# An attention and SwiGLU kernel on one core: fewer, longer dummy products, F's turns and V's projections moved up, a quotient moved to GpSimd, and smaller weight loads at the start

## The chip, the cores and the metric

The kernel runs on one core of one Trainium2 chip. The metric is the device time of one execution in microseconds (us). All runs here are of one core; the granted clock of every run is 0.997 to 1.0. Three runs, with three different kernels, fell to 0.997 at 570.4 to 570.9 us.

The engines are called by the profile's names: PE is TensorE (PEld its weight loads), DVE is VectorE, ACT is ScalarE, POOL is GpSimd, SP is SyncE. GpSimd computes the attention's quotients and also issues nearly all loads.

## The reference

```python
k_proj = np.einsum('ks,bhsd->bhkd', E, k)          # q, k, v: 8 x 8 x 1024 x 64, E, F: 64 x 1024
v_proj = np.einsum('ks,bhsd->bhkd', F, v)
attn   = softmax(q @ k_proj.T / sqrt(64))          # over 64 projected keys
x      = (attn @ v_proj), heads side by side       # 8192 x 512
out    = (silu(x @ w_gate) * (x @ w_val)) @ w_out  # d_ff = 1536
```

## The kernel before

There are 8 batches of two halves of 512 tokens. Steady work is the feed-forward network: per half, 12 features of 128 columns, each with four gate and four value products of 128x512. The attention of the coming half is put into "slots" between them. Only the first batch's attention and its loads can't hide, and the change is all there.

Some words used below: a "turn" is a transpose, done as a product with the identity on TensorE (`u_T` for q, `u_A` for the attention, `turn` for E and F). "Quotient" N(b, u) is the exponentials times the reciprocal of their sum (`u_N`). BD and BDV hold the projected keys and values, AT the turned attention, xT the attention's result; "P V" is the product of attention and projected V. "Gate 1" or "value 4-5" is the load of these features' weights. A load "lands" when its semaphore says that it is complete. An "instruction packet" is a DMA packet that brings the program's own instructions (queue q8 in the profile).

```python
def load_w_gv(c0, c1, which=(0, 1)):      # weights of features c0..c1-1, GpSimd issues
    cs = slice(c0 * P, c1 * P)
    for wsrc, wdst in [((moe_w_gate, wg), (moe_w_val, wv))[i] for i in which]:
        nc.gpsimd.dma_start(out=wdst[:, :, cs], in_=wsrc[:, cs].rearrange(...))

def u_N(b, u, eng=nc.gpsimd):             # the attention's quotient, on GpSimd
    ... eng.tensor_tensor(out=a, in0=ee, in1=rr, op=ALU.mult)

def u_TD(b, ch):                          # q of later batches is transposed by DMA
    nc.sync.dma_start_transpose(out=t[:], in_=qb[b, ch][:]...)

def place(b):                             # slots of batch b's attention
    ...
    put(s0 + (9 if b == 2 else -6), u_TD, b, 0)
    o = 14 if b == 2 else 6
    sa = [s0 + o + 3 * j for j in range(NJ)]       # scores, and quotient one slot later
...
load_w_gv(4, 6)                           # the loads after the start, in this order
load_q(0, 1, hs=(0, 4))
load_w_gv(6, 8)
load_q(0, 1, hs=(4, 8))                   # q's heads 4-7 of the second half
load_w_gv(8, 10); load_w_gv(10, 12)
load_q(1, 0); load_k(1); load_wo(0); load_wo(1)
for i, u in enumerate(range(4, 8)):       # the second half of batch 0
    put(11 + i, u_T, 0, u)                # q's turn on TensorE
    put(13 + i, u_S, 0, u)                # scores
    put(14 + i, u_R, 0, u); put(14 + i, u_N, 0, u)
```

The softmax here doesn't subtract the row's maximum and nothing guards it: scores larger than these inputs give would overflow.

## Time and profile before

| | before |
|---|---|
| median time | 568.79 us (568.78 to 568.80, 3 runs) |
| span of the profiled run | 566.9 us |
| TensorE busy | 560.2 us, 99% |
| first full-width product (feature 2, gate) | 25.07 us |
| from there to the end | 541.8 us |

The table is read from the bottom: after 25 us TensorE does almost nothing but multiply. The prediction below shows the lines.

### The profile page before, as it was taken

To read this page: it belongs to the slowest core of one execution; us is meant where nothing else is said; L and a number is where in the kernel's file an instruction comes from. 1 tells how busy PE (TensorE), PEld (TensorE's weight loads), DVE (VectorE), ACT (ScalarE), POOL (GpSimd) and SP (SyncE) were. 2 spreads that over 40 slices of the span, in tenths; PEclk is the share of its full clock that TensorE was granted. 3 is DMA by queue.
4 is the path that set the end of the run, shared out by engine and by line. 5 is a ranking of instruction groups with operands and counts; after the bars stand their busy time and mean duration, and the time that the engine had idled before them with its cause. 6 is when DMAs were issued, how large, how long until landed. Compare 5 with 4: busy or idle time off the path is not lost.

```text
span 566.9 us, 7938 instructions
## 1 busy us (share of the span) xinstructions
PE 560.2 (99%) x2970; PEld 266.3 (47%) x2970; DVE 339.2 (60%) x576; ACT 236.0 (42%) x417; POOL 110.4 (19%) x124
## 2 busy tenths in 40 slices
PE   8999999999999999999999999999999999999997
PEld 4654444444444444444444444444444444444444
DVE  3786664766476645766466655666547665545550
ACT  3664352444435433443434434354343543443222
POOL 6851250124012400124002230023100220000000
PEclk9999999999999999999999999999999999999999
DMA  9999989729913795029940499105990214100012
GB/s 201 194 200 188 175 126 199 141 57 187 192 50 74 113 196 119 38 57 163 183 83 37 76 185 204 38 19 101 200 183 20 57 38 75 38 37 32 25 38 93
DMA packets 111159, 62.78 MB, mean 111 GB/s; under 512 B 64272, under 2 KB 102416, under 8 KB 111120
## 3 DMA queue, kind: packets, MB, share of 16 engines
q0 software_dynamic: 42896, 29.49, 36.1%
q1 hardware_dynamic: 67392, 31.46, 26.2%
q10 hardware_dynamic: 832, 1.31, 0.8%
q8 instruction: 23, 0.38, 0.3%
q14 instruction: 16, 0.13, 0.1%
HBM read 60.29 MB, written 16.78 MB: 136 GB/s over the span
## 4 chain that ended last, share of the span: by engine, by line
PE 97%; ACT 1%; DVE 1%; issue 0%
PE gps L377 29%; PE yps L415 29%; PE vps L377 29%; PE kvp L150 3%; PE sc L271 2%; PE pv L328 2%; PE warm L513 1%; ACT ee L275 0%; ACT AT L138 0%; DVE BD L138 0%; ACT th L389 0%; PE qTp L237 0%; PE efp L501 0%; PE aTp L317 0%; PE pv L343 0%
## 5 line engine op out<-in xcount | busy, mean ns | idle before, releaser
L396 DVE SCALAR_TENSOR_TENSOR s<-th,gps 128x512 f32<-128x512 f32 x192 | 130.3, 679 | 134.4 <-ACT th L389 134.0
L377 PE MATMUL gps<-xT,wg 128*128 128x512 bf16 (+1 forms) x776 | 197.6, 377 | 0.1
L377 PE MATMUL vps<-xT,wv 128*128 128x512 bf16 (+1 forms) x776 | 197.5, 377 | 0.0
L415 PE MATMUL yps<-wo,hT 128*128 128x512 bf16 (+1 forms) x780 | 194.5, 376 | 0.0
L389 ACT ACTIVATE th<-gps 128x512 f32<-128x512 f32 x192 | 114.6, 597 | 159.0 <-PE gps L377 153.9
L401 DVE TENSOR_TENSOR hT<-s,vps 128x512 bf16<-128x512 f32 x192 | 131.9, 687 | 20.4 <-DVE s L396 0.5
L301 POOL TENSOR_TENSOR AAd<-ee,rr 128x512 bf16<-128x512 f32 x56 | 58.2, 1041 | 342.5 <-issue 180.6
L415 PEld LDWEIGHTS <-hT 128*128 128x128 bf16 x780 | 76.2, 98 | 89.9
L377 PEld LDWEIGHTS <-wv 128*128 128x128 bf16 x776 | 74.0, 98 | 83.3 <-issue 2.9
L377 PEld LDWEIGHTS <-wg 128*128 128x128 bf16 x776 | 74.0, 98 | 81.3 <-issue 1.2
L425 ACT ACTIVATE ysb<-yps 128x512 f32<-128x512 f32 (+1 forms) x65 | 38.4, 590 | 77.7 <-PE yps L415 77.7
L138 ACT CAST xT<-pv 128x512 bf16<-128x512 f32 (+1 forms) x62 | 35.9, 581 | 52.5 <-PE pv L328 50.3
L286 DVE TENSOR_REDUCE zz<-ee 128x8 f32<-128x512 f32 x64 | 43.4, 679 | 22.1 <-ACT ee L275 22.1
L275 ACT ACTIVATE ee<-sc 128x512 f32<-128x512 f32 x64 | 38.2, 597 | 19.8 <-PE sc L271 18.7
L271 PEld LDWEIGHTS <-qTd 128*128 128x128 bf16 x224 | 17.2, 98 | 13.2 <-DMA qTd<-qb 0.2
L328 PE MATMUL pv<-AT,BDV 128*128 128x512 bf16 x60 | 22.4, 379 | 0.1
L271 PE MATMUL sc<-BD,qTd 128*128 128x128 bf16 x224 | 21.6, 219 | 0.0
L288 DVE RECIPROCAL rr<-zz 128x8 f32<-128x8 f32 x64 | 13.0, 203 | 6.6 <-DVE zz L286 0.5
L108 POOL DMA_DIRECT2D qb<-in_q_dram x18 | 16.3, 907 | 1.4 <-POOLq L651 0.8
L150 PE MATMUL kvp<-kb,ET 128*64 128x512 bf16 (+1 forms) x72 | 15.5, 358 | 0.0
L162 DVE CAST BDV<-kvp 64x256 bf16<-64x256 f32 x7 | 3.0, 426 | 20.0 <-ACT ks L158 17.8
L150 PE MATMUL kvp<-vb,FT 128*64 128x512 bf16 x56 | 13.4, 382 | 0.0
(66 smaller groups left out, 137.6 us busy)
## 6 DMA issues: line engine op xcount, KB each, us to landing
out_dram<-ysb SPq DMA_DIRECT2D x63, 256.0 KB, 2.3
qb<-in_q_dram POOLq DMA_DIRECT2D x14, 512.0 KB, 18.1
kb<-in_k_dram POOLq DMA_DIRECT2D x7, 1024.0 KB, 11.0
vb<-in_v_dram POOLq DMA_DIRECT2D x7, 1024.0 KB, 14.5
wo<-in_moe_w_out_dram POOLq DMA_DIRECT2D x2, 768.0 KB, 21.9
wg<-in_moe_w_gate_dram POOLq DMA_DIRECT2D x5, 256.0 KB, 8.4
wv<-in_moe_w_val_dram POOLq DMA_DIRECT2D x5, 256.0 KB, 9.0
kraw<-in_k_dram ACTq DMA_DIRECT2D x2, 512.0 KB, 4.9
```

Of the source, the lines that this page charges most:

```text
L138: (nc.scalar.copy if eng is nc.scalar else eng.tensor_copy)(out=out, in_=in_)
L150: nc.tensor.matmul(out=t[lo : lo + 64, h0:h1].rearrange("p h d -> p (h d)"), lhsT=w[:, j, :], rhs=src[b][:, h0:h1, j, :], start=(j == 0), ...
L271: nc.tensor.matmul(out=ps[:, n, :], lhsT=t[:, n, :], rhs=BD[b % 2][:, 4 * g + n, :], start=True, stop=True)
L275: nc.scalar.activation(out=e[:].rearrange("p h j k -> p (h j k)"), in_=ps[:].rearrange("p a k -> p (a k)"), func=AF.Exp, scale=scale,)
L286: nc.vector.reduce_sum(out=z[:], in_=e[:], axis=AX.X)
L301: eng.tensor_tensor(out=a.rearrange("p j h k -> p h j k"), in0=ee.pop((b, u))[:], in1=rr.pop((b, u))[:].unsqueeze(3).to_broadcast([P, 4, 2 ...
L377: nc.tensor.matmul(out=ps[:, ts], lhsT=(wg, wv)[w][:, kt, f * P : (f + 1) * P], rhs=x[:, kt, ts], start=(kt == 0), stop=(kt == NKT - 1),)
L389: nc.scalar.activation(out=th[:], in_=ps[:], func=AF.Tanh, scale=0.5)
L396: nc.vector.scalar_tensor_tensor(out=s1[:], in0=th[:], scalar=1.0, in1=g[:], op0=ALU.add, op1=ALU.mult)
L401: nc.vector.tensor_tensor(out=hT[c][:, f, :], in0=s1[:], in1=ps[:], op=ALU.mult)
L415: nc.tensor.matmul(out=yy[c][:, cs], lhsT=hT[c][:, f, i * P : (i + 1) * P], rhs=wo[:, f, cs], start=(f == 0), stop=(f == NFT - 1),)
L425: nc.scalar.activation(out=ysb[:, cs], in_=yy[c][:, cs], func=AF.Copy, scale=0.5)
```

## The change

The intent: put fewer instructions into TensorE's stream with dummies of the same length (they keep its clock up), take the copies of F's turn out from between ScalarE's exponentials, project V before the first P V, free VectorE of the last quotient N(0,3) by giving it to GpSimd, and let the weights of features 2 and 3 land separately.

```diff
-        warm(11)                                # bf16, 512 columns each
+        for n in (8, 8, 6):                     # one fp32 product of 64 n columns each
+            warm(n)
         turn(0, "v")
-        warm(4)
+        warm(8)
 ...                                             # two more such places, one dummy dropped
         load_w_gv(1, 2, (1,))
-        load_w_gv(2, 4, (0,))
+        load_w_gv(2, 3)
 ...
         u_KV(0, "k", (4, 8), at="y")
-        warm(1)
+        turn(1, "a", (0,), dve)
         u_KT0((2, 4), "vg", (dve, dve, act, act))
         u_T(0, 1, "a", dve)
         u_T(0, 3, "a", dve)
+        turn(1, "a", (1,))
 ...                                             # both turn(1, ...) removed further down
         u_R(0, 3)
+        u_N(0, 3)                               # GpSimd; was u_N(0, 3, dve)
+        load_w_gv(3, 4)
         u_A(0, 0, act)
-        u_N(0, 3, dve)
         u_V0(0, 2, "y")
+        u_V0(2, 3, "v")
         u_PV2(0, 0, 0, 0, act)
-        u_V0(2, 3, "y")
-        u_A(0, 2, act)
-        u_V0(3, 4, "v")
+        u_A(0, 2, dve)
+        u_V0(3, 4, "y")
 ...
+        f_mm(0, 0, 0, 0)
         u_A(0, 3, act)
-        load_w_gv(2, 4, (1,))
-        f_mm(0, 0, 0, 0)
```

More of the change, by code (lines that the diff above doesn't have):

```diff
@@ L490 @@
         load_k(0, 4, 8)
-        zeros = const.tile([P, CW], BF16, name="zeros")
+        zero32 = const.tile([P, CW], FP32, name="zero32")
+        nc.vector.memset(zero32[:], 0.0)
+        zeros = const.tile([P, 2 * P], BF16, name="zeros")
         nc.vector.memset(zeros[:], 0.0)
@@ L495, with turn @@
         nc.vector.memset(ks[0][64:P], 0.0)
-        def turn(which, at, halves=(0, 1)):
+        def turn(which, at, halves=(0, 1), eng=nc.scalar):
             for half in halves:
@@ L506, in turn @@
                 js = slice(4 * half, 4 * half + 4)
-                copy(nc.scalar, (ET, FT)[which][:, js, :], ps[:])
+                copy(eng, (ET, FT)[which][:, js, :], ps[:])
         def warm(n):
             ps = bank("v", [P, CW], FP32, "warm")
-            for _ in range(n):
+            z = zeros if n < 4 else zero32
+            for _ in range(n if n < 4 else 1):
                 nc.tensor.matmul(
-                    out=ps[:], lhsT=zeros[:, 0:P], rhs=zeros[:],
+                    out=ps[:, 0 : min(64 * n, CW) if n >= 4 else 2 * P],
+                    lhsT=z[:, 0:P],
+                    rhs=z[:, 0 : min(64 * n, CW) if n >= 4 else 2 * P],
                     start=True, stop=True,
@@ L537 @@
         u_KT0((0, 2), "vg", (dve, dve, dve, act))
-        warm(1)
+        warm(4)
         u_S(0, 0, "g")
@@ L542 @@
         load_w_gv(1, 2, (1,))
-        load_w_gv(2, 4, (0,))
+        load_w_gv(2, 3)
         u_T(0, 2, "a", act)
-        warm(2)
+        warm(4)
         u_KV(0, "k", (4, 8), at="y")
-        warm(1)
+        turn(1, "a", (0,), dve)
         u_KT0((2, 4), "vg", (dve, dve, act, act))
@@ L553 @@
         u_N(0, 2)
-        turn(1, "a", (0,))
         u_S(0, 1, "g")
@@ L557 @@
         u_N(0, 1)
-        turn(1, "a", (1,))
         u_S(0, 3, "v")
         u_R(0, 3)
+        u_N(0, 3)
+        load_w_gv(3, 4)
         u_A(0, 0, act)
-        u_N(0, 3, dve)
         u_V0(0, 2, "y")
+        u_V0(2, 3, "v")
         u_PV2(0, 0, 0, 0, act)
-        u_V0(2, 3, "y")
-        u_A(0, 2, act)
-        u_V0(3, 4, "v")
+        u_A(0, 2, dve)
+        u_V0(3, 4, "y")
         u_PV1(0, 0, 2, 0, dve)
```

## The prediction

> **What bounds the kernel now.** I read the page first, then busy time in long stretches, then the chain of waits for the first 25 us, and last each load of the start with its time to landing. The page and the stretches say where a change can matter at all:
>
> ```profile
> span 566.9 us, 7938 instructions
> PE 560.2 (99%) x2970; PEld 266.3 (47%) x2970; DVE 339.2 (60%) x576; ACT 236.0 (42%) x417; POOL 110.4 (19%) x124
> ...
> 15.00:25.00 10.00, 8.85 (x123) 7.10 (x123) 6.95 (x15) 6.89 (x16) 8.85 (x13) 1.00 1.50 193
> 25.00:565.00 540.00, 538.75 (x2772) 252.54 (x2771) 326.71 (x547) 223.56 (x390) 90.92 (x93) 1.00 0.61 107
> ```
>
> In a stretch line the columns are the window, its length, then the busy time of PE, PEld, DVE, ACT and POOL, the granted clock, the DMA share and GB/s. From 25 to 565 us TensorE is busy 538.75 of 540 us at clock 1.00; the list of waits has no wait of TensorE over 0.1 us after 21 us. So 566.9 - 25.07 = 541.8 us after the first full-width product of feature 2 (start 25.07) is product after product, and the change touches none of it. The time moves by what the start of that product moves, one to one, as long as the loads then still arrive.
>
> In the start, the chain of waits (start, length, what) ends so:
>
> ```profile
> 14.94 0.60 ACT ee L275
> 15.54 0.26 ACT FT L138
> 15.80 0.50 ACT ee L275
> 16.30 0.26 ACT FT L138
> 16.57 0.50 ACT ee L275
> 17.07 0.48 ACT AT L138
> 17.55 0.29 ACT BDV L185
> ...
> 23.29 0.39 PE gps L377 x2
> 23.68 0.02 issue
> 23.70 0.61 ACT th L389
> 24.31 0.02 issue
> 24.33 0.70 DVE s L396
> 25.03 0.04 issue
> 25.07 0.38 PE gps L377
> ```
>
> The reader is to see ScalarE as the limit from 14.9 to 17.8: the two copies of F's turn (0.26 each) stand between the exponentials, and the first evicted attention (AT) and V projection (BDV) queue behind. At the end, tanh (0.61) and the VectorE product (0.70) free the bank that feature 2 needs.
>
> A second limit hardly shows in the chain: the loads. The share of the DMA engines is at its top from 2 us on. The landings, each from the issue line of a small window, are (issue + time to landing): V heads 0-3 at 5.66 + 9.9 = 15.5, heads 4-5 at 16.9, heads 6-7 at 18.1, gate feature 0 at 18.8, value feature 0 at 8.65 + 12.5 = 21.2, gate 1 at 11.24 + 10.1 = 21.4, value 1 at 14.26 + 7.7 = 22.0. The first use of value 0 is the product at 21.36:
>
> ```profile
> 21.36 0.60 PE L377 MATMUL vps<-xT,wv 128*128 128x256 bf16 x4
> ```
> ```profile
> wv<-in_moe_w_val_dram POOLq DMA_DIRECT2D x1, 128.0 KB, 12.5
> ```
> ```profile
> q0 software_dynamic: 818, 0.20, 172.8%
> q8 instruction: 1, 0.02, 4.9%
> ```
>
> So that weight is only 0.2 us early. Value 0 comes 2.3 us after gate 0, though the same 128 KB elsewhere take about 0.6 (gate 1 to value 1: 21.4 to 22.0). The last fence, DMA packets between 19.0 and 20.2 us, shows why I suspect this is no matter of bytes: one packet of an instruction queue, 0.02 MB, took 4.9% of 16 engines x 1.2 us, 0.94 us of one engine, in the middle of these loads. A load has landed only when all its engines are through, so that engine's lag delays value 0, gate 1 and value 1.
>
> **What the Trainium skill says.** "FP8 and Floating Point Precision", section "TensorE Precision Notes": a true fp32 product is four passes through the array. The trace agrees roughly: E's eight fp32 turns of 64 columns take 1.07 us, 133 ns each, where four passes of 64 columns at 2.4 GHz (the clock of the next page) are 107. "TensorE: Matmul & The Clock Gate", Part 1: the array starts at half clock and is released after a busy window of some 3.4 us. The trace agrees: eleven dummies of 512 columns take 4.88 us, 444 ns each, and full-width products later advance by 0.86 / 4 = 216 ns. "DMA: Bandwidth & Descriptors", "Issuing engines are not separate DMA queues": all issuers share the 16 engines; the instruction packet above fits. Its table "Specifications" puts full rate at 512 B and up; here loads of one feature (256 B packets) take about 0.74 us of data, loads of two (512 B) 1.34, so two halves cost 2 x 0.74 - 1.34 = 0.14 more.
>
> **The change, part by part.**
> Dummies: 11 + 4 + 1 + 2 + 1 = 19 products of 512 columns become 3 + 1 + 1 + 1 = 6 fp32 products of 22, 8, 4 and 4 times 64 columns. At four passes, 22 x 64 x 4 = 5632 = 11 x 512: the same time in the first group, the same for 8, 4 (for 2), and 1024 instead of 512 column passes for the first 4; the last one is gone. That extra 0.21 us falls in TensorE's 0.72 us wait for BD before 10.90: free. The memset ahead is twice as large in bytes: 0.48 us (the row of that size, BD's) instead of 0.27, so the dummies start about 0.2 us later and end near 6.1 to 6.4 instead of 6.1; E's turns start at 6.12 now, and K's copies hold the projection till 8.0 of its 8.2. Cost 0 to 0.2 us. Removed are 13 products and 13 weight loads, 26 instructions of TensorE's stream.
>
> F's turns: the first goes between k's second projection (ends 13.18; F landed at 5.00 + 8.1 = 13.1) and the kT products at 13.63, its copy on VectorE done by 13.9, when BD begins: free. The second falls where TensorE waits for BD before 14.56. Both 0.26 us copies leave the exponentials: these end near 16.5 instead of 17.1, AT at 17.0 instead of 17.55, BDV of pairs 0-1 at 17.3 instead of 17.83. That is 0.5 us.
>
> V projections ahead: pair 2 is projected at 16.9 (its V lands then), P V of pairs 0-1 at 17.4 instead of 17.88. The second attention's turn follows at 17.9, when GpSimd has its quotient (17.65), and VectorE copies it (0.4) as N(0,3), 1.13 us, has gone to GpSimd (there done at 18.7 + 1.0 = 19.7). It is ready at 18.5 instead of 19.65. Pair 3 must wait for V at 18.1; its BDV at 18.95, P V 1 of pair 3 at 19.0, its xT at 19.7. The first gate products then end at 19.9 instead of 21.14: 1.2 us of work gained up to here.
>
> Then value 0 is needed at 20.3 and, if it lands as before, is there at 21.2. From there: value 0 at 21.2 to 21.65, gate 1 to 22.1, P V to 22.3, its xT (0.58 after 0.2 of latency) at 23.05, the second gate half ends at 23.3 instead of 23.68, and tanh, product and feature 2 follow at 24.85. Gain 0.2 us. If the instruction packet no longer stands in the way, value 0 lands near 19.6, gate 1 at 20.4, value 1 at 21.1; the same steps give feature 2 at 24.0: gain 1.05.
>
> Slices: gate 2 and value 2 alone land earlier (some 0.6 us) than a load of two; features 3 and later come 0.27 us later and are issued behind N(0,3). Value 2 lands at 24.65 and is wanted at 25.93 now, gate 4 at 26.0 and 28.5, so even a start 1 us earlier has room. Cost 0.
>
> Where the instruction packet falls is the choice. It follows TensorE's instruction count; at 19.14 about 290 traced TensorE instructions have begun. The stream is 26 shorter, but the work runs up to 1.2 us ahead by then, and the two nearly cancel: I expect it at 18.9 to 19.6 again, still among the first weights. So more weight on the small gain: 0.2 (likeliest), 0.4 if the packet falls just behind value 0, 1.05 if past all four. Weighted 0.55, 0.25, 0.15 and 0.05 for a loss of 0.3: 0.35 us.
>
> **Rivals.**
> 1. The loads take over wholly (gain 0 to 0.2, 568.6 to 568.8): for it, value 0 is only 0.2 us early; against it, the packet's place is not fixed.
> 2. The packet moves out of the way: 567.7. For it, fewer TensorE instructions; against it, the earlier work.
> 3. The fp32 dummies last longer or do not count as activity, or the later memset misses the busy window: the clock rises 3.4 us later, E's turns, dummies and k's projection run at half speed. About 1.5 us more, of which some 0.9 hides behind value 0: 569.3. Against it, four passes keep the array as busy, and the dummies start 1.4 us in, still before the last 3.4 us ahead of the rise at 6.1.
> 4. VectorE becomes the limit: it already carries three reductions and reciprocals from 15.57 to 18.06, and takes a copy of F's turn and one of AT on top. Those fall at 13.5 and after 18.06, so I see at most 0.1 us.
>
> **Range and chances.** 568.79 - 0.35 = 568.4. The range takes in rival 2 at its low end and a small loss at its high end: 567.7 to 568.9. Two per cent is 11.4 us, more than nearly all that the start has to give or a cold clock could cost: within 2% is 0.985.
>
> **What would show it.** Right: the exponentials without a copy between them, ending near 16.5; first gate products ending near 19.9; then TensorE waiting for value 0 until about 21.2; feature 2 at 24.8; 541.8 us after it. Wrong: no instruction packet among the first weights and value 0 at 19.6 (rival 2); full clock only past 6.5 us, or E's turns later than 6.5 (rival 3); a TensorE wait for a weight after feature 2 (the slices come too late).

## More of the kernel before

Of the kernel before, after 19.5 us (who waited for what: us in total, times, longest):

```profile
PEld L271 <- DMA qTd<-qb: 0.2, 1, 0.2
```

It is the weight load of batch 2's first scores, which takes q as a DMA has transposed it (`qTd`), at 104.84 us; the transfer landed at 104.80. Its wait tells that the transfer came just in time, though the products show no gap.

## The result, and the profile after

The changed kernel took 568.99 us (median of 4 runs: 569.17, 569.14, 568.82, 568.84), the kernel before 568.78 in the same rounds. Ratios are the mean time of one kernel's fast runs over that of the other's of the same rounds, so not quite the ratio of the medians: 1.0004, interval 0.9986 to 1.0021. Later (r_after, chip 2) it was 568.97 (568.33 to 569.42) against 568.79, ratio 1.0003. It is the same time, or 0.2 us more, where 0.4 less was forecast. The range of 567.7 to 568.9 missed it by 0.1.

First the chain of waits of the changed kernel (start, length, what):

```profile
15.66 1.53 ACT ee L275 x3
17.19 0.48 ACT AT L138
17.67 0.28 ACT BDV L185
...
19.33 1.03 POOL AA L301
20.36 0.76 POOL wg L118
21.13 0.74 POOL wv L118
...
25.51 9.19 DMA qb<-in_q_dram
34.70 0.05 issue
34.74 0.40 PE qTp L237 x4
```

The three exponentials now stand together (1.53 us), as the change wanted. But the chain leaves the computing engines: it goes through GpSimd's last quotient (N(0,3), `AA`), then its issue of the loads one after another, then a load of q, to a turn on TensorE at 34.74. The chain of before has no load in it. Its shares by engine, from its page, and then those of after:

```profile
PE 97%; ACT 1%; DVE 1%; issue 0%
```
```profile
PE 95%; DMA 2%; POOL 1%; ACT 1%; DVE 0%; issue 0%
```

Now the stretch from feature 2's first product to 35 us, before and then after. The columns are the window, its length, then busy us of PE, PEld, DVE, ACT, POOL with instructions, clock, DMA share, GB/s:

```profile
25.07:35.00 9.93, 9.93 (x58) 5.00 (x58) 8.29 (x13) 4.51 (x9) 5.48 (x7) 1.00 1.45 196
```
```profile
24.65:35.00 10.35, 9.72 (x57) 4.82 (x57) 8.71 (x14) 4.75 (x9) 7.21 (x10) 1.00 1.36 179
```

Feature 2 starts at 24.65 instead of 25.07: the start did gain 0.42 us. But before, TensorE was busy in all of its 9.93 us, and after, in 9.72 of 10.35. The waits of the changed kernel after 19.5 us name it, for products and weight loads:

```profile
PE qTp L237 <- DMA qb<-in_q_dram: 0.6, 1, 0.6
```
```profile
PEld L237 <- DMA qb<-in_q_dram: 0.8, 1, 0.8
PEld L271 <- DMA qTd<-qb: 0.4, 1, 0.4
```

The book of starts, from the timelines of both kernels: feature 2 is 0.42 us ahead; the turn of q's heads 4-7 comes at 34.74 instead of 34.37, the line of before that follows, so the lead is a lag of 0.37. The 0.8 us between are the wait of its weight load.

```profile
34.37 0.39 PE L237 MATMUL qTp<-ident_bf,qb 128*128 128x128 bf16 x4
```

Then a wait for GpSimd's quotients near 40.7 adds some 0.1; at the first scores of batch 1 the lag is 0.49 (61.62 against 61.13), and it stays so to the end (567.4 against 566.9).

Why the load was late shows in the DMA queue. Stretches of 1 us, before and then after, same columns:

```profile
22.00:23.00 1.00, 1.00 (x12) 0.89 (x11) 0.74 (x3) 0.35 (x1) 1.00 (x2) 1.00 1.45 198
...
24.00:25.00 1.00, 0.98 (x9) 0.72 (x8) 0.67 (x1) 0.72 (x2) 0.69 (x2) 1.00 1.45 196
25.00:26.00 1.00, 0.93 (x5) 0.45 (x5) 0.90 (x3) 0.17 (x1) 0.68 (x1) 1.00 1.45 196
```
```profile
22.00:23.00 1.00, 0.98 (x10) 0.73 (x9) 0.85 (x3) 0.59 (x1) 1.00 (x2) 1.00 1.19 112
...
24.00:25.00 1.00, 0.90 (x8) 0.54 (x6) 0.90 (x2) 0.60 (x1) 1.00 (x3) 1.00 1.22 146
25.00:26.00 1.00, 1.00 (x7) 0.44 (x5) 0.99 (x2) 0.29 (x1) 1.00 (x2) 1.00 1.17 150
```

The queue moved 196 GB/s without a break before; after, it fell to 112 and then to about 150. GpSimd's timelines say why (start, length, engine, line), before and then after:

```profile
16.64 2.04 POOL L301 TENSOR_TENSOR AA<-ee,rr 128x512 bf16<-128x512 f32 x2 [0.84 <-ACT FT L138]
18.63 0.80 POOL L118 DMA_DIRECT2D wv<-in_moe_w_val_dram  x1
```
```profile
17.33 3.04 POOL L301 TENSOR_TENSOR AA<-ee,rr 128x512 bf16<-128x512 f32 x3 [0.31 <-ACT ee L275]
20.32 0.81 POOL L118 DMA_DIRECT2D wg<-in_moe_w_gate_dram  x1
```

After the quotients, the next load is issued at 20.32 instead of 18.63, and two loads of half the size stand before features 4 and 5 instead of one: gate 4-5 is issued at 21.85 instead of 19.43 and lands at 27.2 instead of 26.0. All that follows is late by the same 1.24 us. Then q's heads 4-7 are late by 2.05: 34.70 (issued 25.51, 9.19 us) instead of 32.65 (issued 23.08, 9.57). The extra 0.8 goes with an instruction packet of 0.94 us that started at 32.48: q landed 2.12 us after the load before it (value 6-7, 32.58). The kernel before has such a packet as well, at 31.55, but there q landed 1.33 us after value 6-7. The packets' lines, from 31 to 33 us before and from 32 to 33.5 after:

```profile
q8 instruction: 1, 0.02, 2.9%
```
```profile
q8 instruction: 1, 0.02, 3.9%
```

With 1.33 us, q would have landed near 33.9 (an estimate), just when its turn was due: at 33.95, which is 34.37 less the lead of 0.42. So in this trace the 1.24 us used up q's slack, and the packet turned that into a wait. e11 is the counterpart: there a packet (31.22) delayed the same load, 2.23 us after the one before, but with the queue on time q landed at 33.28, 0.68 before its turn. e2 shows the other half: no packet fell on q's load there (1.37), and the late queue alone made TensorE wait.

### The profile page after: what moved, and what is told of

Its sections match the earlier page's. It is cut to its first block, busy times and chain, and to the rows that moved or that the text cites. A ratio compares the mean times of both kernels' runs of the same rounds, so it can differ in the third digit from the quotient of the medians.

```text
span 567.4 us, 7930 instructions
## 1 busy us (share of the span) xinstructions
PE 560.9 (99%) x2963; PEld 266.5 (47%) x2963; DVE 339.2 (60%) x578; ACT 235.5 (42%) x415; POOL 113.0 (20%) x127
## 4 chain that ended last, share of the span: by engine, by line
PE 95%; DMA 2%; POOL 1%; ACT 1%; DVE 0%; issue 0%
PE yps L415 29%; PE vps L377 28%; PE gps L377 28%; PE kvp L150 3%; PE sc L271 2%; PE pv L328 2%; DMA qb<-in_q_dram 2%; PE warm L517 1%; POOL wg L118 0%; POOL wv L118 0%; ACT ee L275 0%; POOL AA L301 0%; PE efp L503 0%; PE qTp L237 0%; PE aTp L317 0%
```

## The experiments

All results were correct. The median of each is set beside the kernel before in the same rounds. Single runs of one kernel differ by up to 1.3 us here even without the three runs at 0.997 (one cause is when TensorE's clock rises, see e1 and e9), so the traces carry the argument and the medians only support it.

| run | median us (range) | before us | feature 2 starts (traced run) |
|---|---|---|---|
| e1_dummies | 568.85 (568.48 to 569.22) | 568.76 | 24.93 |
| e2_bf16 | 568.38 (568.37 to 568.88) | 568.76 | 24.72 |
| e3_pairs | 568.38 (568.18 to 568.72) | 568.76 | 24.46 |
| e4_late | 569.40 (568.69 to 569.93) | 568.76 | 24.75 |
| e5_pairs_s2 | 568.47 (568.18 to 568.76) | 568.83 | 24.70 |
| e6_before_s2 | 568.69 (568.59 to 570.39) | 568.83 | 25.02 |
| e7_ndve | 569.19 (568.40 to 570.56) | 568.83 | 25.58 |
| e8_pairs_s2_short | 568.22 (568.07 to 568.31) | 568.83 | 24.64 |
| e9_many | 568.34 (568.25 to 569.56) | 568.79 | 25.90 |
| e10_merge | 568.25 (568.04 to 568.36) | 568.79 | 24.76 |
| e11_turns | 568.49 (568.25 to 568.75) | 568.79 | 24.66 |
| r_after | 568.97 (568.33 to 569.42) | 568.79 | 24.80 |

The theory: the start gains, but the loads that feed later work became late, and deadlines further on take the gain back. The rivals: the fp32 dummies cost the start; N(0,3) on GpSimd alone does it; the instruction packet delays q; the waits named only stand in for others.

**e1_dummies.** The kernel before, with the dummies of the changed one.

```diff
-        warm(11)
+        for n in (8, 8, 6):
+            warm(n)                 # fp32, and the three later places likewise
```

> The kernel before with the fp32 dummies alone. Theory A (the dummies cost the front 0.46 us, as after shows: k's first projection at 8.69 instead of 8.23): k's projection at 8.6 to 8.7, feature 2 at 25.4 to 25.5 instead of 25.07, no lost time later, time 569.1 to 569.3. The instruction packet moves behind value 0 (to about 20.4), value 0 lands near 19.6. Theory B (the front has slack before value 0, so the dummies are free): feature 2 at 25.1, time 568.8.

It took 568.85, which is theory B's time, but neither theory's feature 2 came: 24.93. k's first projection began at 7.96, not 8.6, since the first group of dummies was done at 5.8 and not at 6.5. In the traces of the changed kernel and its variants that same group took 5.06, 4.09 and 5.06 us (after, r_after, e5): the number of column passes is fixed, and the granted clock rises at another moment in each run: in the traces that record it between 4.1 us (e6) and 7.6 (e5), in one at 10.7 (e9). So the 0.46 us by which k's projection was late in the first trace of the changed kernel is not a constant of the dummies. What is constant is their start, 1.46 instead of 1.20 us. The instruction packet did not move to 20.4 either: it started at 19.03, value 0 landed in time (19.26) and gate 1 late (21.16).

**e2_bf16.** The changed kernel with the old dummies.

```diff
-        for n in (8, 8, 6):
-            warm(n)
+        warm(11)                    # bf16 again, and the later places likewise
```

> The changed kernel with the old bf16 dummies. Theory A: k's projection is back at 8.2 and all that depends on it 0.46 earlier, but TensorE's stream has 33 instructions more ahead, so the instruction packet falls at 18.2 to 18.9 instead of 19.73 and value 0 or gate 1 lands after 20.5; feature 2 at 24.2 to 24.6; the second load of q's second half (heads 4-7) still lands after 33.9 and TensorE waits for it, so the time stays at 568.7 to 569.1. Theory B (the start alone sets the time): 568.79 less what feature 2 gains, 568.2 or less.

The trace went as theory A says from the loads on: gate 1 landed at 21.39 and was waited for (0.38 us), q's heads 4-7 at 34.41, and batch 1's scores had 0.41 us of weight-load wait; but the instruction packet fell at 19.22, later than expected. (The profile lists 12 instructions more than in the changed kernel, not 33: see the dummies under "Why the prediction was wrong".) Value 6-7, the load before q's, was already 1.72 us late (33.04 against 31.32). That run, 568.88, was the slowest of five. The others took 568.37 to 568.45, below theory A and above theory B, and no trace of them exists. So the medians say that the old dummies are 0.6 us better inside the changed kernel, and why the other four were faster stays open.

**e3_pairs.** The slices undone, N(0,3) still on GpSimd.

```diff
-        load_w_gv(2, 3)
+        load_w_gv(2, 4)
 ...
-        load_w_gv(3, 4)
```

> The changed kernel with gate and value of features 2 and 3 in one load each again, both at the place of the first slice. Theory A (the slices and their place behind N(0,3) let the load queue run short): the load rate from 21 to 29 us is near 196 GB/s again, q's heads 4-7 land at 32.5 to 33.5, TensorE's wait of 0.63 us at 34.1 is gone; feature 2 at 24.65, time 568.3 to 568.5. Theory B (the slices are harmless, N(0,3) on GpSimd or the instruction packet delays q): q lands at 33.9 or later, time 568.8 to 569.1.

Theory A held: q's heads 4-7 landed at 32.34, the rate stayed at 195 to 198 GB/s, the wait at 34 us was gone, and the median was 568.38. An early start is not what saved it: r_after's k projection began as early (8.03, here 8.00), and it waited for q. The stretch that fell to 150 GB/s in the changed kernel:

```profile
25.00:26.00 1.00, 1.00 (x6) 0.42 (x5) 0.90 (x3) 0.47 (x1) 0.75 (x2) 1.00 1.45 195
```

The traced run itself took 568.57, though batch 1's scores were 0.55 us ahead of before. It lost 0.44 at 104.81 us, the deadline at which the kernel before already had its weight load waiting:

```profile
PE sc L271 <- DMA qTd<-qb: 0.3, 1, 0.3
```

**e4_late.** The changed kernel, heads 4-7 asked for one slot later.

```diff
+            d = i + (i > 1)
-            put(11 + i, u_T, 0, u)
+            put(11 + d, u_T, 0, u)          # scores, sums and quotients likewise
```

> The changed kernel, with the turns and scores of heads 4-7 of the second half one slot later. Theory A (the wait for q's heads 4-7 is where the gain went): loads land as in the changed kernel (q at 34.7), but the turn is asked for after 34.9, no wait over 0.2 us; feature 2 at 24.65; time 568.3 to 568.5. Theory B (that wait only stands in for another one, such as the attention quotients behind it): the loss moves to the attention turns near 40 us, time 568.8 to 569.1.

Neither: the wait at 34 us was gone, as A says, and the time rose, to 569.40. The chain of this run:

```profile
42.62 19.18 DMA qTd<-qb
61.81 0.05 issue
61.85 0.40 PE sc L271 x4
```

Batch 1's transposed q became the next deadline. TensorE waited 1.09 us for it. In the traced changed kernel this DMA landed at 61.57, 0.05 us before the scores that need it: the wait at 34 us hid it. The late loads thus have two deadlines, and one load queue behind both: q of batch 1 landed at 42.6 here, at 42.5 in the changed kernel, at 40.7 before.

**e5_pairs_s2.** e3_pairs with batch 2's scores one slot later.

```diff
-            o = 14 if b == 2 else 6
+            o = 15 if b == 2 else 6
```

> The changed kernel with features 2 and 3 loaded in pairs (as e3_pairs) and batch 2's scores one slot later. Theory A (three deadlines in a row eat the gain: q's heads 4-7 at 34 us, batch 1's transposed q at 61.6, batch 2's at 104.8; the last already binds the kernel before): no wait of TensorE over 0.2 us after 30 us, the lead of some 0.5 us at the scores of batch 1 survives to the end, time 568.0 to 568.4. Theory B (104.8 is only where jitter shows; something else sets the end): the loss comes back elsewhere, time 568.4 or more.

Its trace has no wait of TensorE over 0.2 us after 30 us, and the lead at batch 1's scores (0.31 us) is there at the end (0.30). The median, 568.47, is just outside A's range and inside B's, and not below e3_pairs (568.38; another chip). So the trace supports the third deadline, the medians show no gain from moving it.

**e6_before_s2.** The same edit in the kernel before.

> The kernel before with batch 2's scores one slot later: the control. Theory A (the kernel before has no slack at 104.8 but is not held there by more than a weight load's 0.24 us): time 568.6 to 568.9, as before, perhaps with more spread. Theory B (later scores help by themselves): 568.5 or less.

568.69 against 568.83: within the spread. The later scores don't help by themselves.

**e7_ndve.** The changed kernel with slices, N(0,3) on VectorE again.

```diff
-        u_N(0, 3)
+        u_N(0, 3, dve)
         load_w_gv(3, 4)
```

> The changed kernel with the quotient N(0,3) back on VectorE, the slices kept. Theory A (the slices and N(0,3) on GpSimd together empty the load queue; without N(0,3) the loads of feature 3 are issued 1.0 us earlier): gate 4-5 lands near 26.2 instead of 27.2, q's heads 4-7 at 33.0 to 33.7, batch 1's transposed q near 60.5; feature 2 later than in the changed kernel by 0.3 to 0.8 as VectorE's copies wait for N(0,3); time 568.5 to 568.9. Theory B (the slices alone empty the queue): gate 4-5 at 27 or later and q at 34 or later still.

Theory A's loads: the next load was issued at 19.27, gate 4-5 landed at 25.9, q's heads 4-7 at 32.55, with no wait for them. So the slices do no harm if GpSimd is free to issue a microsecond earlier. The price is on VectorE, which holds a copy behind the quotient:

```profile
PE pv L355 <- DVE AT L138: 1.1, 1, 1.1
```

Feature 2 came at 25.58, 0.9 later than in the changed kernel, and the time was 569.19, above the expected range by 0.3.

**e8_pairs_s2_short.** e5_pairs_s2 with 20 instead of 22 times 64 columns of first dummies.

```diff
-        for n in (8, 8, 6):
+        for n in (8, 8, 4):
```

> As e5_pairs_s2, with the first group of dummies cut from 22 to 20 times 64 columns (0.43 us at half clock), so that E's turns wait for E and not for dummies when the clock is released late. Theory A (in a run with a late release the dummies hold the front by up to 0.4 us): E's turns at 5.8 to 6.1 in every run, median 0 to 0.2 below e5_pairs_s2 and less spread. Theory B (the front is not what bounds the first weights): the same as e5_pairs_s2.

568.22, all five runs between 568.07 and 568.31, where every one of the eleven runs of before took at least 568.60. The ratio is 0.9986, interval 0.9974 to 0.9998: small, and still the same time by the 2% rule, but the only interval here that leaves out 1. It is 0.25 below e5_pairs_s2 in the same rounds, with less spread, as theory A says. The changed kernel was not in these rounds; its medians in others were 568.99 and 568.97. E's turns began at 5.89. Its stretch from feature 2 shows what the changed kernel lacked, a TensorE without a gap and a full queue:

```profile
24.64:35.00 10.36, 10.36 (x60) 5.17 (x60) 8.73 (x14) 4.95 (x10) 5.96 (x8) 1.00 1.45 197
```

It still waits for one weight, gate 1, 0.40 us at 21.35.

**e9_many.** e8 with the first dummies as 40 bf16 products of 128 columns: as many passes and more instructions (77 if an fp32 product is one; by the profile 34 products and 34 weight loads).

```diff
-        for n in (8, 8, 4):
-            warm(n)
+        for _ in range(40):
+            nc.tensor.matmul(out=ps[:, 0:P], lhsT=zeros[:, 0:P], rhs=zeros[:, 0:P], ...)
```

> As e8_pairs_s2_short, but the first group of dummies as 40 bf16 products of 128 columns instead of 3 fp32 ones: the same 5120 column passes, 77 more instructions of TensorE. Theory A (the instruction packet follows TensorE's instruction count): it starts between 16.5 and 18.5 instead of 19.1, V's heads 6-7 or gate 0 lands 0.9 us or more later than in e8 (17.99, 18.71), the first gate products end 0.5 to 1.2 us later, time 568.4 to 569.1. Theory B (the packet's place has nothing to do with the count): it stays at 18.9 to 19.9, gate 1 or value 1 is the late one, time as e8, 568.2.

The instruction packet did move, from 19.08 to 16.54. From 16 to 18 us e8's DMA view has none, e9's has one:

```profile
q8 instruction: 1, 0.02, 3.0%
```

And the late load moved with it: V's heads 6-7 took 11.7 us instead of 10.9 (landed 18.79, not 17.99), while gate 1, late in e8 (21.30), landed at 20.87 and value 1 at 21.60. So more TensorE instructions bring this packet earlier, and it delays the loads it falls among. The kept traces add that the second packet stands behind 229 to 235 TensorE weight loads in all 14 of them, though its time runs from 27.71 us (e9) to 34.29 (e10). That supports the count. The first, however, stands behind 141 to 158 in twelve traces, 109 in e9 and 132 in e10, so it is not at a fixed count. The time, 568.34, is just below A's range; what the late V load cost the four fast runs no trace shows. The traced run was the slow one of five (569.56), by its clock: e9's second group of dummies, then e8's:

```profile
7.14 2.08 PE L517 MATMUL warm<-zero 128*128 128x512 f32 x2
```
```profile
6.98 1.12 PE L517 MATMUL warm<-zero 128*128 128x512 f32 x2
```

At 2.08 us it ran at half clock, and so did k's projection (1.78 instead of 1.06). It is the late clock that rival 3 of the prediction feared, here with bf16 dummies and in the one run of five that was traced, and feature 2 came 1.26 us later than in e8.

**e10_merge.** e8 with V's pairs 2 and 3 in one projection and one P V.

```diff
-        u_V0(2, 3, "v") ... u_V0(3, 4, "y") ... u_PV1(0, 0, 2, 0, dve) ... u_PV1(0, 0, 3, 0, act)
+        u_V0(2, 4, "v") ... u_PV2(0, 0, 1, 0, act)
```

> As e8_pairs_s2_short, with V's pairs 2 and 3 projected together and their P V in one: 34 instructions of TensorE fewer before the first gate products, and these products behind the last turn of the attention. Theory A (the packet follows the count): it starts after 20.0, all four first weights land by 21.0, no wait for a weight, feature 2 at 24.1 to 24.4, time 567.7 to 568.1. Theory B: the packet stays near 19.1, gate 1 lands after 21, feature 2 at 24.6, time 568.2 to 568.5.

As its expectation says, the first gate products also moved behind the attention's last turn. It took 568.25, as e8: theory B by its numbers. The packet started at 19.35, not after 20, gate 1 landed at 21.43, and feature 2 stayed at 24.76. Removing 34 instructions moved it by 0.3 us only. Where exactly it is triggered is not settled.

**e11_turns.** The kernel before with F's turns moved, nothing else.

```diff
+        turn(1, "a", (0,), dve)       # for warm(1), after k's second projection
 ...
+        turn(1, "a", (1,))            # after u_T(0, 3, ...); both old places removed
```

> The kernel before with F's turns moved alone. Theory A (they take 0.5 us out of ScalarE's chain, but the loads hold what follows): exponentials end near 16.5 instead of 17.07, feature 2 at 24.7 to 25.0, and the scores of batch 2 wait for their transposed q near 104.8: time 568.6 to 568.8. Theory B (ScalarE's chain sets the time): 568.3 or less.

The chain of this run, next to the six lines that the prediction shows of before:

```profile
14.74 0.37 ACT FT L138
15.12 1.53 ACT ee L275 x3
16.65 0.48 ACT AT L138
```

The last attention copy starts at 16.65 instead of 17.07, and feature 2 at 24.66 instead of 25.07. In this run the lead of 0.42 us lasted to the end; the weight load at 104.3 waited 0.12. So A's start was right, and A's loss at batch 2's deadline did not come in this trace. The median, 568.49, lies between both theories. This one part, alone, is worth 0.3 us by the medians; the interval of the ratio (0.9983 to 1.001) doesn't tell it from nothing.

**r_after.** The changed kernel again.

> The changed kernel once more, on the same chip and in the same rounds as the others: 568.8 to 569.2 by every theory; the wait for q's heads 4-7 and the transposed q of batch 1 at its deadline should show again.

568.97, with an early clock this time (the dummies took 4.09 us). It repeats the story: a wait of 0.36 us for gate 1 at 21.5, a lead of 0.27 at feature 2, q's heads 4-7 at 34.55, again behind a packet (32.24), with 0.33 us of wait, a lag of 0.31 at batch 1's scores, batch 1's transposed q landing at 61.27 with its weight load waiting until 61.31, and 0.29 us lost at the end.

## Why the prediction was wrong

It said 568.4, within 567.7 to 568.9, and the time was 568.99. That it would be within 2% was right. Its steps:

- **"541.8 us after the first full-width product of feature 2 ... and the change touches none of it"** is the step that failed. The changed kernel needed 567.4 - 24.65 = 542.75. TensorE's products show no wait there in the kernel before because its loads were in time, and the change moved the loads. The sentence had its own condition, "as long as the loads then still arrive", and only weights were checked against it.
- **"Slices ... Cost 0"** is where the condition was checked too narrowly: value 2 and gate 4 against their uses. They did arrive in time. Not checked were q's heads 4-7 (due at 33.95 with the new lead, landed at 34.70), nor the DMA queue's depth: the next load is issued behind N(0,3), and two issues of 0.75 us each stand before features 4 and 5 instead of one. Nor was the second instruction packet, which added 0.8 us to that load. "Features 3 and later come 0.27 us later" was 1.24 us from feature 4 on. e3 and e7 show that it takes both parts, the slices and the quotient on GpSimd; either one alone leaves q in time (32.34 and 32.55).
- **Dummies, "Cost 0 to 0.2 us":** their start is 0.26 later in every trace with the new dummies. The rest depends on when the clock rises: the cost at k's projection was 0.46 in the first trace and nothing visible in the second. "26 instructions" fewer are 14 by the profile, 7 products and 7 weight loads (2963 instead of 2970 of each), as it lists an fp32 product as two. The 107 ns for a turn of E are an estimate from figures of the Trainium skill (four passes, "FP8 and Floating Point Precision", "TensorE Precision Notes"; 2.4 GHz, "TensorE: Matmul & The Clock Gate", Part 1); the trace's 133 is 1.07 us over eight, while their starts are 0.11 us apart, which is nearer.
- **F's turns, 0.5 us:** right in mechanism, 0.42 in size (e11).
- **V projections ahead:** the first gate products were to end 1.2 us earlier. By the timelines they ended at 19.77 + 0.89 = 20.66 in the first trace and at 20.26 in r_after, where before has 20.70 + 0.60 = 21.30: 0.64 us with the late front, 1.04 with the early one.
- **Value 0 to land at 21.2:** it landed at 19.3. The instruction packet fell at 19.73, within 0.13 us of the forecast of 18.9 to 19.6, but behind value 0; it hit value 1 (21.82). What the first gate products waited for was not a weight: the last of them began at 20.39, after ScalarE's copy of xT. (N(0,3) on GpSimd was done at 20.37, just before its turn.) Feature 2 at 24.65 was forecast at 24.85, which is near by luck: the wait for value 0 didn't come, and the first gate products ended 0.76 later than forecast.
- **Rivals:** none of the four had a later load take the start's gain. The list of what would prove the prediction wrong names "a TensorE wait for a weight after feature 2 (the slices come too late)". It was right about the kind of wait, and wrong about which data.

Where the gain went is thus settled for the traced runs: 0.42 us gained in the start, about 0.8 given back at q's heads 4-7 (34 us), by a load queue 1.24 us late and a packet on top, another 0.1 at the quotients behind it. Had that wait not been, batch 1's transposed q would have taken it (e4). Open are the rate of 150 GB/s with few loads outstanding, the exact trigger of the instruction packets, and the four untraced runs of e2, which had the same late loads in the code and were as fast as e3. V's projections moved up were not run alone.

## What to carry to other kernels

A busy TensorE says that transfers come in time, not that they have time to spare: before moving an issue, list the next loads in queue order, each with its landing and its first use, down to the deadline with the least slack, and read the waits of the weight loads, too. An engine that issues loads is part of the load path: an operation moved onto it, or a load cut in two, delays the issue of every later load. Whether they also land late depends on the queue: here either alone was absorbed (e3, e7), and both together let it run short and cost 1.24 us. Leave room for an instruction packet, too, which here added about 0.8 us to a load. When two deadlines share one queue, removing the first wait exposes the second; mend the queue and not the wait.

## What the Trainium skill lacked or had wrong

- "Runtime: NRT & Kernel Launch", "Instruction fetch mechanics", says that instructions are refilled in blocks of 16 KiB over a DMA queue, and that crossing a block is "mostly hidden". It doesn't say what that costs the loads. Here a packet of 16 KB took 0.94 us of one engine; q's heads 4-7 landed 2.12 us after the load before instead of 1.33, and V's heads 6-7 at 18.79 instead of 17.99 when more TensorE instructions brought the packet there (e9).
- "DMA: Bandwidth & Descriptors", "Anatomy of one DMA", fits a load as about 2.0 us plus bytes over 436 GB/s, which makes an estimated 2.6 us for 256 KB. In the short queue of the changed kernel gate 4-5, with two loads of 128 KB issued just before it, took 5.4 us from issue to landing, at 146 to 154 GB/s of all queues; the page has nothing on a queue that nearly runs dry.
- "TensorE: Matmul & The Clock Gate", Part 1, says that the moment when the clock rises varies by some 500 ns from run to run. Here the granted clock rose between 4.1 and 7.6 us, once at 10.7 (e9, where k's projection took 1.78 instead of 1.06 us); one group of fp32 dummies took 4.09 us in one run and 5.06 in another of the same kernel. That is more than this figure; the page's own 6, 11 or 14 slow products in runs of one kernel fit better.
- "FP8 and Floating Point Precision", "TensorE Precision Notes", has four passes for a true fp32 product, and the time agrees: 5632 passes at 1.2 GHz, the half clock of "TensorE: Matmul & The Clock Gate", are an estimated 4.7 us for a measured 5.06. It doesn't say that the profile lists such a product as two matmuls: three dummies stand as x6.
